# A tiled expert network on one core: half of the low-half weight tiles made by a VectorE subtraction instead of a ScalarE negation and an adding DMA

## Chip, core and metric

The kernel runs on one core of a Trainium2 chip. Its metric is the device time of one execution in microseconds (us). Three runs of the kernel before took 1112.21, 1112.51 and 1117.79 us; the median is 1112.51 us.

## What is computed

The program has three stages, each of which needs the whole of the one before it.

```python
attn_out = _attn_ref(q, k, v)                 # 4 x 8 heads, 768 tokens, head size 64, decaying state
x = attn_out.transpose(0, 2, 1, 3).reshape(3072, 512)
h = x @ w_in                                  # 512 -> 2048
x = np.where(h > 0, h, np.exp(np.minimum(h, 0)) - 1) @ w_out     # 2048 -> 512
logits = x @ w_gate                           # 3072 x 8 experts
...                                           # all logits sorted; a token goes to the best expert that
...                                           # still has room (3072 / 8 = 384 tokens each)
for e in range(8):                            # each expert: 512 -> 1024 -> 512 on its 384 tokens
    h = np.maximum(x[mask_e] @ w1[e], 0.0)
    out[mask_e] = h @ w2[e]
```

Which expert a token gets depends on an order over all logits, so the products are done in more than one float32r pass: each operand is kept as a high half (its rounding to float32r) and a low half (what the rounding left), and a product is the sum high x high + low x high + high x low.

## The kernel before, in words

**Order of the work.** `body` builds the program with generators (threads). Each yields the engine that it wants and the tiles that it needs, and `Sched` picks the thread that can go first by the times that `Plan` keeps: `Plan.cost` and `Plan.pe_cost` say how long an instruction takes, and `Plan.note` (line 153) books it. For a DMA `note` adds the bytes divided by a rate to one common DMA clock (line 168). The result is one fixed order on each engine; on the chip an engine works its queue in that order, and an instruction whose operand is late holds all behind it. So a changed cost in `Plan` moves instructions everywhere a DMA is waited for. All recorded operations have line 199 in the profile, since `Engine.__getattr__` issues them; tiles tell them apart.

**First part (0 to about 690 us).** Attention (`sc`, `A`, `py`, `pu`) and the first network (`ph`, `e`, `gH`/`gL`, `px`) over 12 blocks of 256 tokens. Its weights come in as 64-bit numbers (`rw`), are narrowed by three VectorE operations each, and split into `w1H`/`w1L`, `w2H`/`w2L`. From about 100 us TensorE (PE) is full.

**Expert part (about 690 us to the end).** `route(ph)` (line 850) finds, for one expert after the other, which expert fills next and with which tokens. It is a chain on VectorE (DVE): six digits, each with a compare `c`, a product `pc` on PE, `nums`, `num`, a second product into `pc`, `ind`, a product `pj`, `jd` and the next `xd`. It ends with the expert's number `es` and, through `listing`, its token list `idx`. Phases 0 to 6 run this chain, phase 7 is a short rest. `load_experts` (line 1095) lets the SP queue read `es` and then load the expert's weights as eight tiles of 512 KB, `e1R` and `e2R` in turn, into a ring of five buffers (`RAWS`, tag `raw`). `splits` (line 1116) makes the halves of each tile: ACT copies `x` to the high half `h`, ACT writes `-h` to the low half `l`, and a DMA from the GpSimd (POOL) queue adds `x` to `l` in place. The ring buffer is free again when that DMA has read it. `fetch` (line 1142) gathers the expert's tokens (`xg`) by indirect DMA, PE transposes them (`pt`), ACT and DVE split them (`xTH`, `xTL`). `ffn_first` (PE, `eh`), `ffn_mid` (ACT `hH`, DVE `hL`), `ffn_second` (PE, `po`) and `outs` (`o`, scatter to `out_dram`) do the expert's network: 96 `eh` and 72 `po` matmuls for each expert. The digit matmuls of routing stand in PE's queue between them.

The lines that matter: 

```python
h, l = (wp.tile(shp, F32R, tag=t, ...) for t in tags)     # splits, line 1125
copy("ACT", h, x)
ACT.activation(l, h.bitcast(F32), AF.Copy, scale=-1.0)
POOL.dma_start(l.bitcast(F32), x, accum_op=OP.add)
```

Of the kernel before, what the change touches and what calls it, by code (L numbers as in the profile page):

```python
# [12 lines left out]
F32 = mybir.dt.float32  # L13
# [4 lines left out]
AF = mybir.ActivationFunctionType  # L18
OP = mybir.AluOpType
# [68 lines left out]
class Plan:  # L88
# [64 lines left out]
    def note(self, eng, op, out, ins):  # L153
        o = out.tensor.name
        start = max([self.free[eng]] + [self.ready.get(x.tensor.name, 0.0) + self.gap(x.tensor.name, eng) for x in ins])
        if eng != "PE" or self.writer.get(o) != "PE":
            start = max(start, self.used.get(o, 0.0) + 140)
        if eng == "PE":
            end = start + self.pe_cost(op, ins, start)
            if start > self.free[eng] + 20:  # L160
                end += 100
        else:
            end = start + self.cost(eng, op, out, ins)
        self.free[eng] = end
        self.writer[o] = eng
        if "dma" in op:
            nb = self.size(out if out.space != "DRAM" else ins[0]) * P * 4
            self.dma = max(self.dma, end + 600) + nb / 360.0
            end = self.dma + 1300
        for x in ins:  # L170
            k = x.tensor.name
            self.used[k] = max(self.used.get(k, 0.0), end)
        self.used[o] = max(self.used.get(o, 0.0), end)
        self.ready[o] = max(self.ready.get(o, 0.0), end) if "dma" in op or eng == "PE" else end
# [107 lines left out]
def on(eng, *needs, when=None, rank=None):  # L282
    return eng, needs, when, rank
# [3 lines left out]
def body(ctx: ExitStack, tc, qkv, w_in, w_out, w_gate_t, w1, w2, cst, rc, rmat, out, dbg=None):  # L287
# [3 lines left out]
    PE, ACT, DVE, POOL, SP = (  # L291
        Engine(e, n, plan)
        for e, n in ((nc.tensor, "PE"), (nc.scalar, "ACT"), (nc.vector, "DVE"), (nc.gpsimd, "POOL"), (nc.sync, "SP"))
    )
# [20 lines left out]
    def copy(eng, o, i):  # L315
        if eng == "ACT":
            ACT.activation(o, i, AF.Copy)
        else:
            engines[eng].tensor_copy(o, i)
# [793 lines left out]
    def set_free(p):  # L1113
        return did["rest"] > 4 if p == 0 else did["late_x"] if p == 1 else did["p2e"] >= nf * (p - 1)

    def splits():
        for p in range(E):
            for q in range(8):
                i = q // 2
                yield on("ACT", when=lambda: did["loaded"] > 8 * p + q and set_free(p) and (p > 0 or q < 2 or did["gather"]))  # L1120
                x = weights[(p, q)]
                nm, shp = (("w1", [P, KD, 256]), ("w2", [P, 2, DM]))[q % 2]
                tags = [f"{nm}{h}{i + 4 * (p % 2)}" for h in "HL"]
                yield on("ACT", x, wp.slot(tags[0]))
                h, l = (wp.tile(shp, F32R, tag=t, name=f"{nm}{t[2]}{p}_{i}") for t in tags)
                copy("ACT", h, x)
                yield on("ACT", h)
                ACT.activation(l, h.bitcast(F32), AF.Copy, scale=-1.0)
                yield on("POOL", l)
                POOL.dma_start(l.bitcast(F32), x, accum_op=OP.add)  # L1130
                weights[(p, q)] = (h, l)
                did["split"] += 1

# [143 lines left out]
    sched.add(4, ffn_second())  # L1277
    sched.add(5, ffn_first())
    sched.add(6, splits())
    sched.add(7, load_experts())  # L1280
    sched.run()
# [35 lines left out]
```

## Time and profile before

| | us |
|---|---|
| median of three runs | 1112.51 |
| the profiled execution, its own time | 1109.6 |
| its span, first to last instruction | 1107.8 |
| PE busy in the span | 1010.9 (91%) |
| DVE busy | 736.8 (67%) |
| ACT busy | 422.1 (38%) |
| POOL busy | 258.0 (23%) |

The profiled execution lies 2.9 us under the median of the runs, and 1.8 us of it lie outside its span. A page of the profile gives busy times for each engine, the span in 40 slices of 27.7 us, the DMA queues, and the chain of waits that ended last. Queries on the trace give the same for a stretch of time, group the instructions by tile and shape, and list who waited for whom.

### The profile page before, as it was taken

Reading aid. Unit: us, or ns where it says so; the run is one execution under the profiler, and the core shown is the slowest. Engines: PE = TensorE matmul, PEld = TensorE weight load, DVE = VectorE, ACT = ScalarE, POOL = GpSimd, SP = SyncE. Lnnn points to the kernel's source line nnn. Section 1 sums busy time; section 2 is a strip of 40 time slices with the busy share of each in tenths; the row PEclk is TensorE's granted clock in tenths of the full one; section 3 lists DMA queues with packets and bytes.
Section 4 is the critical chain, followed back from the end, with each engine's and each line's share of the span. In section 5 each row is a group of like instructions: output and inputs, shape, how many; then the busy total and the mean of one; then the engine's idle time right before and its main releaser. Section 6 shows DMA issues by size and latency. Waiting matters only on the chain.

```text
span 1107.8 us, 17734 instructions
## 1 busy us (share of the span) xinstructions
PE 1010.9 (91%) x6899; PEld 847.4 (76%) x6899; DVE 736.8 (67%) x1853; ACT 422.1 (38%) x639; POOL 258.0 (23%) x250
## 2 busy tenths in 40 slices
PE   4779899999999999999999999959798898996996
PEld 3657687978787878787879899748586676786885
DVE  4989877898989888866574655567465565662210
ACT  3536423323232333323233344055353545545531
POOL 4665421211211212110000000032232324333321
PEclk8789999999999999999999999989898989998999
DMA  9743232020202020201010000099797979989860
GB/s 317 258 158 115 101 109 96 1 95 2 96 1 87 9 81 16 74 24 65 32 57 1 20 1 12 20 261 241 192 238 194 243 195 224 252 235 259 195 151 29
DMA packets 60582, 131.80 MB, mean 119 GB/s; under 512 B 4689, under 2 KB 29265, under 8 KB 60369
## 3 DMA queue, kind: packets, MB, share of 16 engines
q1 hardware_dynamic: 47440, 84.52, 22.7%
q0 software_dynamic: 13056, 46.14, 19.2%
q8 instruction: 54, 0.88, 0.3%
q14 instruction: 32, 0.25, 0.1%
HBM read 84.51 MB, written 12.58 MB: 88 GB/s over the span
## 4 chain that ended last, share of the span: by engine, by line
PE 61%; DVE 15%; DMA 13%; issue 6%; ACT 2%; POOL 1%; SPq 0%; POOLq 0%; DVEq 0%; ACTq 0%
PE px L199 19%; PE ph L199 18%; PE eh L199 8%; PE po L199 8%; DVE junk L199 6%; PE py L199 4%; DMA e2R<-in_w_dram 3%; DVE n_rw L199 3%; DMA rw<-in_moe_w_in_dram 3%; DMA e1R<-in_w_dram 2%; DVE e L199 2%; DMA xg<-xd,idx 2%; DMA w1L<-e1R 2%; PE sc L199 1%; DVE gL L199 1%
## 5 line engine op out<-in xcount | busy, mean ns | idle before, releaser
L199 PE MATMUL ph<-yH,w1H 128*128 128x256 f32 x768 | 219.9, 286 | 8.1 <-DVE e L199 8.1
L199 PE MATMUL ph<-yL,w1H 128*128 128x256 f32 x768 | 216.0, 281 | 0.8 <-DVE yL L199 0.8
L199 PE MATMUL ph<-yH,w1L 128*128 128x256 f32 x768 | 215.9, 281 | 0.0
L199 PEld LDWEIGHTS ph<-yH,w1H 128*128 128x128 f32 x768 | 145.7, 190 | 14.5 <-DVE e L199 7.3
L199 PEld LDWEIGHTS ph<-yH,w1L 128*128 128x128 f32 x768 | 145.7, 190 | 1.6
L199 PEld LDWEIGHTS ph<-yL,w1H 128*128 128x128 f32 x768 | 145.5, 190 | 1.3 <-DVE yL L199 1.3
L199 PE MATMUL px<-w2H,gH 128*128 128x512 f32 x332 | 136.3, 411 | 8.8 <-DMA rw<-in_moe_w_in_dram 5.1
L199 PE MATMUL px<-w2H,gL 128*128 128x512 f32 x332 | 132.4, 399 | 1.7 <-DVE gL L199 1.7
L199 PE MATMUL px<-w2L,gH 128*128 128x512 f32 x332 | 132.9, 400 | 0.0
L199 DVE SCALAR_TENSOR_TENSOR junk<-x,wgb 128x512 f32<-128x512 f32 x160 | 128.0, 800 | 5.0 <-ACT x L199 1.2
L199 ACT ACTIVATE e<-ph 128x512 f32<-128x512 f32 x96 | 56.8, 592 | 195.5 <-PE ph L199 195.5
L199 DVE SCALAR_TENSOR_TENSOR hL<-eh,hH 128x384 fp32r<-128x384 f32 x64 | 35.6, 557 | 97.6 <-ACT hH L199 97.0
L199 ACT ACTIVATE gH<-e 128x512 fp32r<-128x512 f32 x83 | 52.3, 631 | 123.6 <-DVE e L199 115.0
L199 DVE SCALAR_TENSOR_TENSOR junkw<-wsum,wgb 128x512 f32<-128x512 f32 x128 | 89.4, 698 | 11.0 <-POOL wsum L199 8.4
L199 PE MATMUL eh<-xTH,w1H 128*128 128x384 f32 x256 | 91.5, 358 | 1.6 <-ACT xTH L199 1.6
L199 PE MATMUL eh<-xTL,w1H 128*128 128x384 f32 x256 | 90.1, 352 | 0.0
L199 PE MATMUL eh<-xTH,w1L 128*128 128x384 f32 x256 | 89.9, 351 | 0.0
L199 PE MATMUL po<-w2H,hH 128*128 128x512 f32 x192 | 80.5, 419 | 10.0 <-ACT hH L199 10.0
L199 PEld LDWEIGHTS px<-w2H,gH 128*128 128x128 f32 x332 | 63.3, 191 | 25.3 <-ACT gH L199 9.4
L199 POOL TENSOR_TENSOR qk<-qk,csb 128x512 f32<-128x512 f32 x23 | 32.0, 1392 | 212.3 <-DMA qk<-in_qkv_dram 212.3
L199 PE MATMUL po<-w2L,hH 128*128 128x512 f32 x192 | 79.8, 416 | 0.0
L199 PE MATMUL po<-w2H,hL 128*128 128x512 f32 x192 | 79.7, 415 | 0.0
(168 smaller groups left out, 1930.2 us busy)
## 6 DMA issues: line engine op xcount, KB each, us to landing
e1R<-in_w_dram SPq DMA_DIRECT2D x32, 512.0 KB, 6.3
e2R<-in_w_dram SPq DMA_DIRECT2D x32, 512.0 KB, 6.6
w1L<-e1R POOLq DMA_DIRECT2D x32, 512.0 KB, 7.3
w2L<-e2R POOLq DMA_DIRECT2D x32, 512.0 KB, 7.6
kv<-in_qkv_dram SPq DMA_DIRECT2D x24, 512.0 KB, 5.0
qk<-in_qkv_dram SPq DMA_DIRECT2D x23, 512.0 KB, 4.5
rw<-in_moe_w_in_dram SPq DMA_DIRECT2D x16, 512.0 KB, 10.3
rw<-in_moe_w_out_dram SPq DMA_DIRECT2D x16, 512.0 KB, 8.9
```

Source lines behind the costliest of these rows:

```text
L199: r = real(*args, **kw)
```

## The change

In `splits`, a tile whose index `i` is even (`i` runs 0 to 3 for each of `w1` and `w2`) gets its low half from one DVE subtraction `l = x - h`; for an odd `i` ACT and the adding DMA make it as before. So 32 of 64 negations (ACT) and 32 of 64 adding DMAs (POOL queue) go, and 32 subtractions of 128 x 1024 elements (DVE) come. In `Plan.note` the rate at which the planner lets a DMA move bytes changes from 360 to 150 (bytes per ns) for direct DMAs of POOL, and to 310 for all others.

```diff
@@ Plan.note
-            self.dma = max(self.dma, end + 600) + nb / 360.0
+            self.dma = max(self.dma, end + 600) + nb / (150.0 if op == "dma_start" and eng == "POOL" else 310.0)
@@ splits
                 copy("ACT", h, x)
-                yield on("ACT", h)
-                ACT.activation(l, h.bitcast(F32), AF.Copy, scale=-1.0)
-                yield on("POOL", l)
-                POOL.dma_start(l.bitcast(F32), x, accum_op=OP.add)
+                if i % 2 == 0:
+                    yield on("DVE", h)
+                    DVE.tensor_sub(l, x, h.bitcast(F32))
+                else:
+                    yield on("ACT", h)
+                    ACT.activation(l, h.bitcast(F32), AF.Copy, scale=-1.0)
+                    yield on("POOL", l)
+                    POOL.dma_start(l.bitcast(F32), x, accum_op=OP.add)
```

Both edits move instructions. First DVE in the third digit of routing phase 2, while expert 1's weights come in (`c_2`, `nums_2`, `ind_2`, `jd_2` are the digit's chain; `hL` and `xTL` belong to the expert network). Before:

```order
L199 TENSOR_TENSOR c_2_7714<-xd_1_7712,rmb 128x768
L199 TENSOR_TENSOR nums_2_7733<-pc_2_7725,rmb 128x32
L199 SCALAR_TENSOR_TENSOR hL_7723<-eh_7_7686,hH_7722 128x384
L199 TENSOR_REDUCE num_2_7745<-nums_2_7733 128x8
L199 SCALAR_TENSOR_TENSOR w_2_7749<-xd_1_7712,dig_7502 128x24
L199 TENSOR_TENSOR ind_2_7753<-pc_2_7725,rem 32x8
L199 TENSOR_REDUCE jd_2_7760<-pj_2_7756 128x1
```

and now:

```order
L199 TENSOR_TENSOR c_2_7721<-xd_1_7719,rmb 128x768
L199 TENSOR_TENSOR w1L_2_7729<-e1R_2_7539,w1H_2_7728 128x1024
L199 TENSOR_TENSOR nums_2_7750<-pc_2_7735,rmb 128x32
L199 TENSOR_REDUCE num_2_7752<-nums_2_7750 128x8
L199 TENSOR_TENSOR w2L_2_7733<-e2R_2_7615,w2H_2_7732 128x1024
L199 SCALAR_TENSOR_TENSOR w_2_7762<-xd_1_7719,dig_7507 128x24
L199 TENSOR_TENSOR ind_2_7764<-pc_2_7735,rem 32x8
```

Two subtractions stand between the steps of one digit. Of the 32, one stands in the token listing after phase 0, three in phase 1 and four in each of phases 2 to 6; the other eight come after routing.

Second PE around the product `pn` of the last routing chain, phase 6 (the digit behind `eh` and `po` is the expert, the next one the piece `f` of `eh`). Before:

```order
L199 MATMUL po4_2_9662<-w2L4_3_9530,hH39_10121 128x512
L199 LDWEIGHTS rmb_6594
L199 MATMUL pn6_10154<-g6_10140,rmb_6594 128x384
L199 MATMUL po4_2_9662<-w2H4_3_9529,hL39_10122 128x512
L199 MATMUL eh5_0_10168<-xTH5_9889,w1H5_0_9741 128x384
```

and now:

```order
L199 MATMUL po5_1_10149<-w2H5_0_9801,hH41_10152 128x512
L199 LDWEIGHTS rmb_6594
L199 MATMUL pn6_10185<-g6_10167,rmb_6594 128x384
L199 MATMUL po5_1_10149<-w2L5_0_9802,hH41_10152 128x512
L199 MATMUL po5_1_10149<-w2H5_0_9801,hL41_10153 128x512
L199 MATMUL po5_2_10150<-w2H5_0_9801,hH41_10152 128x512
L199 MATMUL po5_2_10150<-w2L5_0_9802,hH41_10152 128x512
L199 MATMUL po5_2_10150<-w2H5_0_9801,hL41_10153 128x512
L199 MATMUL eh5_2_10195<-xTH5_9893,w1H5_1_9870 128x384
```

Behind `pn` of phase 6 there stood 288 `eh` and 217 `po` matmuls, now 264 and 203: 24 and 14 have moved ahead of it. Between `pn` of phases 1 and 2 stood 87 `eh` and 65 `po`, now 61 and 54; in the four stretches after that together 360 and 276, now 397 and 301.

Third SP near the start of the program, where it loads the first network's weights (`rw`) and the attention blocks (`qk`, `kv`). Before:

```order
L199 DMA rw_211<-in_moe_w_in_dram 128x4x256
L199 DMA rw_213<-in_moe_w_in_dram 128x4x256
L199 DMA qk_234<-in_qkv_dram 128x1024
L199 DMA kv_235<-in_qkv_dram 128x1024
```

and now:

```order
L199 DMA qk_223<-in_qkv_dram 128x1024
L199 DMA kv_224<-in_qkv_dram 128x1024
L199 DMA rw_229<-in_moe_w_in_dram 128x4x256
L199 DMA rw_231<-in_moe_w_in_dram 128x4x256
```

One block's load goes ahead of a weight load there, and behind one at a second place; the rest of SP's order, the whole expert part in it, is the same. On PE, DVE, ACT and POOL the order of the first 130 us or so changes with it, and DVE takes two `w1L` subtractions and two of the `rw` scalings of that part from POOL (ACT takes two more scalings), and hands one `qk` and one `kv` product to POOL.

## Rows read from the trace of the kernel before

**Rows 1.** The page, parts 1 and 2: busy times; 40 slices, DMA in tenths.
```profile
PE 1010.9 (91%) x6899; PEld 847.4 (76%) x6899; DVE 736.8 (67%) x1853; ACT 422.1 (38%) x639; POOL 258.0 (23%) x250
...
DMA  9743232020202020201010000099797979989860
```

**Rows 2.** Stretches: routing phases 0 to 6 (from m<-lg on), two more.
```profile
core 0: us, PE busy (x) PEld busy (x) DVE busy (x) ACT busy (x) POOL busy (x), PEclk, DMA share, GB/s
690.50:728.20 37.70, 35.81 (x207) 26.05 (x205) 23.67 (x103) 5.40 (x7) 1.15 (x1) 1.00 0.20 70
728.20:762.70 34.50, 24.54 (x158) 19.22 (x159) 22.46 (x95) 15.44 (x20) 9.55 (x10) 0.85 1.00 242
762.70:809.80 47.10, 41.15 (x239) 33.13 (x238) 26.50 (x107) 21.95 (x28) 13.72 (x17) 0.89 0.82 210
809.80:856.60 46.80, 40.74 (x250) 33.39 (x249) 26.84 (x109) 22.34 (x29) 13.60 (x17) 0.93 0.85 220
856.60:903.70 47.10, 40.45 (x241) 32.03 (x240) 26.51 (x108) 22.02 (x28) 13.63 (x17) 0.93 0.85 212
903.70:945.40 41.70, 38.25 (x244) 30.92 (x243) 26.29 (x108) 23.10 (x30) 14.20 (x17) 1.00 0.93 233
945.40:986.90 41.50, 39.16 (x245) 32.42 (x243) 24.76 (x97) 23.01 (x30) 14.22 (x17) 0.96 0.90 225
986.90:1030.00 43.10, 34.37 (x188) 29.62 (x187) 16.59 (x57) 21.84 (x29) 13.35 (x14) 0.88 1.01 268
1030.00:1064.00 34.00, 34.00 (x171) 30.77 (x170) 6.12 (x11) 21.15 (x27) 10.47 (x15) 1.00 0.89 205
```

**Rows 3.** DMA queues from 720 to 1064 us: packets, MB, share of 16 engines.
```profile
q0 software_dynamic: 12362, 43.83, 59.4%
q1 hardware_dynamic: 25888, 34.08, 30.1%
```

**Rows 4.** The SP queue's own waits: us in total, times, longest.
```profile
SPq L199 <- DMA w1L<-e1R: 119.1, 18, 10.8
SPq L199 <- DVE sel L199: 74.8, 4, 26.0
```

**Rows 5.** Who waited for whom in the expert part, same columns.
```profile
DVE hL L199 <- ACT hH L199: 97.0, 37, 15.5
...
ACT w1H L199 <- DMA e1R<-in_w_dram: 42.0, 8, 11.6
```

**Rows 6.** The chain that ended last: start us, us, link.
```profile
832.10 10.96 DMA e2R<-in_w_dram
```

**Rows 7.** Busy time of stretch 20 to 120 us, columns of rows 2.
```profile
20.00:120.00 100.00, 79.72 (x540) 65.77 (x540) 96.03 (x124) 49.72 (x85) 64.31 (x42) 0.85 0.51 181
```

**Rows 8.** DVE groups, first 130 us: count, busy us, mean ns.
```profile
L199 DVE TENSOR_SCALAR rw<-rw 128x512 f32<-128x512 f32 x2 | 2.0, 980 | 0.0
...
L199 DVE TENSOR_TENSOR kv<-kv,csb 128x512 f32<-128x512 f32 x1 | 1.4, 1450 | 0.0
```

**Rows 9.** keepL, subtraction of two SBUF inputs: ns min/median/max, first, last start.
```profile
L199 DVE TENSOR_TENSOR keepL<-e,keepH x13: 691/693/694, 647.6 to 686.1; 128x512 fp32r<-128x512 f32 x13
```

**Rows 10.** The same for gL in the first 130 us, where POOL computes too.
```profile
L199 DVE TENSOR_TENSOR gL<-e,gH x9: 677/685/1784, 41.0 to 123.0; 128x512 fp32r<-128x512 f32 x9
```

**Rows 11.** Groups in the expert part, columns as in rows 8.
```profile
L199 DVE SCALAR_TENSOR_TENSOR hL<-eh,hH 128x384 fp32r<-128x384 f32 x64 | 35.6, 557 | 97.6 <-ACT hH L199 97.0
L199 ACT ACTIVATE w1L<-w1H 128x1024 fp32r<-128x1024 f32 x32 | 33.8, 1058 | 0.7
```

**Rows 12.** DVE in time, a routing digit: start us, us, instruction, idle before.
```profile
836.02 0.19 DVE L199 TENSOR_TENSOR nums<-pc,rmb 128x32 f32<-128x32 f32 x1 [0.71 <-PE pc L199]
...
836.85 0.15 DVE L199 TENSOR_TENSOR ind<-pc,rem 32x8 bf16<-32x8 f32 x1 [0.31 <-PE pc L199]
```

**Rows 13.** The chain in the stretch where PE is never idle.
```profile
1030.59 4.24 PE eh L199 x24
1034.83 4.20 PE po L199 x18
```

## Prediction

> **What bounds the kernel now.** Begin with the page: PE is busy 91% of the span, DVE 67%, and the DMA slices are low in the middle but 7 to 9 tenths from about 690 us on [rows 1]. So the place to read is the expert part, and the view to read it in is a table of stretches, one for each routing phase [rows 2]. Between 762.7 and 903.7 us a phase takes 47 us; the two after that take 41.7 and 41.5. In the stretch from 1030 us, where routing is over and the weights are in, PE is never idle at the full clock. Before it PE loses time: summed over the seven stretches from 728.2 to 1030, their lengths less PE's busy time make 301.8 - 258.7 = 43.1 us, and a granted clock of 0.85 to 0.96 in six of them adds about 19.6 us (busy time times what the clock lacks). These 63 us are all that the part can give.
>
> Who takes them? The 16 DMA engines are 82% to all but fully occupied [rows 2], and more by POOL's queue than by the loads: in 344 us it has 59.4%, the loads' queue 30.1% [rows 3]. That is 204.3 us for 43.83 MB, so 2.44 us of all 16 engines for one adding DMA of 0.524 MB if its bytes cost as much as the queue's others, against 1.59 us for a load. SP, which issues the loads, waits 119.1 us for the adding DMAs of `w1` tiles to give ring buffers back, and 74.8 us for routing [rows 4]. Late loads of `w1` tiles hold ACT for 42.0 us, and while ACT's queue stands, so does its `hH`, for which DVE waits 97.0 us in all [rows 5]. One link of the chain shows a late load: issued at 832.10, it is waited for over 10.96 us [rows 6]. Routing is the other pacemaker: a digit's steps on DVE and PE answer each other, and all other DVE work stands in between.
>
> **The change, part by part.** I make the sum against the profiled execution, 1109.6 us, which lies 2.9 us under the median of the runs.
>
> *The first part.* Stretch 20 to 120 us has DVE at 96% [rows 7]. The new order gives DVE two subtractions (0.69 each, as `keepL` [rows 9]) and two scalings of 0.98, and takes away two products, one of 1.45 [rows 8] and one that I count as 0.69 like a subtraction of its size: **+1.2 us**. PE idles 20 us in the same 100, so the reordered loads can also give some back or cost more: I keep -5 to +6.
>
> *The subtraction.* No row has one of 1024 columns. With 512 columns it takes 693 ns [rows 9], and a DVE operation of 384 columns (`hL`) takes 557 ns [rows 11], so a column costs about 1.06 ns and 1024 make 1.23 us. Beside POOL's arithmetic the same operation reached 1784 ns [rows 10], 1.1 us more. Bounds: 0.7 and 3.6 us (twice the worst). I take **1.23**, since POOL only issues DMAs and clears one column in the expert part. The Trainium skill (SBUF — State Buffer, Who interferes with whom) says that a VectorE instruction with two SBUF inputs contends with a GpSimd instruction that reads SBUF, and infers that descriptor writing is not hit; the trace agrees with its first half, with 1784 ns where POOL computes, and no row shows the second. If issuing did block it, 24 subtractions at 1.1 us more would add 26 us and the sum would come to about nothing.
>
> *What of it lies on the path.* 24 subtractions come before routing ends: one in the listing ahead of phase 1, three in phase 1, four in each of phases 2 to 6. They stand in the waits of a digit, which under load are some 0.3 to 0.7 us long [rows 12]. So about half of each, 0.6 us, is hidden, and 0.6 is paid: 2.4 us a phase.
>
> *The phases without the adding DMAs.* 32 of them go: 32 x 2.44 = 78 us of 308 us of DMA time, a quarter. Half the ring buffers come back after the subtraction instead of after a DMA's landing. Then the stalls by late loads should mostly go, and a phase is DVE's work plus the waits of the bare chain. DVE is busy 26.2 us in the mean of phases 2 to 6, and in phase 0, which ran with DMA at 0.20, it idled 37.7 - 23.7 = 14.0 us [rows 2]. That makes 40.2, with the subtractions 42.6. Phase 1 had few stalls by loads and gets 3 x 0.6 = **+1.8 us**. The cover for half of each subtraction is the wait for PE's answer; where PE answers at once it is paid in full.
>
> *What PE does meanwhile.* An `eh` matmul takes 4.24/24 = 0.177 us and a `po` 4.20/18 = 0.233 [rows 13]. PE's order has 24 `eh` and 14 `po` fewer behind the last routing phase: 7.5 us of work moved ahead into stretches where PE now idles. Its price there is PE's time: in phases 3 to 6 the mean busy time is 39.65 us, and 37 `eh` and 25 `po` more over the four add 3.1, together 42.75, a little over DVE's 42.6. So phases 2 to 6 make 42.6 + 4 x 42.75 = 213.6 us against 224.2 today: **-10.6 us**.
>
> *The tail.* From 986.9 to the span's end are 120.9 us. The 7.5 us are gone from it, and the first stretch there has 43.10 - 34.37 = 8.7 us of idle PE and 34.37 x 0.12 = 4.1 us of clock, with DMA at 1.01 [rows 2]; I take three quarters of these 12.8 us back, 9.6. **-17.1 us.** The clock's levels are 1.2 and 2.4 GHz; it fell in this part after PE had stood, so it comes back with the stall.
>
> *Costs at nothing.* ACT loses 32 negations of 1.06 us [rows 11]; it is busy 22 to 23 us of a phase, so they pay only by letting `hH` go sooner. POOL loses 32 DMA issues; it is busy some 14 us of a phase [rows 2].
>
> Sum: 1.2 - 10.6 + 1.8 - 17.1 = -24.7 us, 1084.9 for the profiled execution; with 2.9 for the median, **1088 us**. The terms' bounds (first part -5 to +6, hiding all or nothing of 24 subtractions, the tail's stall wholly or by half back) give this case 1075 to 1104.
>
> **The rivals.** *PE becomes the bound.* The subtractions vanish in the waits, DVE idles less, and a phase is as long as PE's work. By matmul busy time there is no room for this (42.75 us). By weight loads there is: in phases 3 to 6 they are busy 32.2 us on average, and where PE never idles they fill 30.77 of 34.00, 90.5% [rows 2], so the work is worth 35.6 us, with 3.1 more 38.7, say 39. Then phases 2 to 6 give 195 - 224.2 = -29.2, phase 1 nothing, the tail -7.5 - 12.8 = -20.3, the first part +1.2: -48.3, **1064 us**. For it: the digit waits are many and the planner places by readiness. Against: DVE's 14 us of waits in phase 0, with hardly any other work. The Trainium skill (Perfetto Trace Analysis, Identifying the Most-Contended Engine) says that matmul busy time is a poor measure of headroom and weight-load busy time a good one; by the first this rival could not be, by the second it ends near 1064. The trace agrees as far as it goes: from 1030 us on PE counts as busy for all of 34.00 us, at a rate of matmuls that phases 2 to 6 don't reach.
>
> *The phases stay.* What lengthens phases 2 to 4 is DVE's own queue, not DMA: they keep their mean of 44.84, plus 2.4. That is +12, +1.8, +1.2 and -17.1: -2.1, **1110 us**. For it: phases 5 and 6, at 41.6, had DMA at 0.9 too.
>
> *DVE as the new holder (slower).* A subtraction waits on DVE for ACT's copy, thus for the load, and holds the digit behind it, `hL` and `xTL`, and with them PE and SP (which waits for routing). Then nothing is hidden and the stalls remain: phases 2 to 6 at 44.84 + 4 x 1.23 = 49.8, +24.7; phase 1 +3.7; first part +1.2; tail -17.1: +12.5, **1125 us**. It decides from where phases 2 to 6 average 47.3 us, 2.4 over today, since the other terms give 12.2 us for five. Against: loads will land sooner, and ACT's in-order queue already held `hL` in this way.
>
> That the change doesn't do what it says is small: the subtraction frees its ring buffer, but the odd tiles still need their adding DMA, and a phase that waits for one of these waits as before. It lies between the forecast and 1110.
>
> **How the numbers follow.** A measurement here can tell about 0.5%, 5.6 us, from no change. Forecast 0.52, PE as the bound 0.25, the phases stay 0.13, DVE as holder 0.10. The first two are faster by over 0.5%: 0.77; the third is the same: 0.13; the last slower: 0.10. The range runs from just under the PE case to the case of no change, 1062 to 1112, and leaves out the slower case and some of the faster one's low end.
>
> **What would show it.** Right: `w1L<-e1R` and `w2L<-e2R` as DVE operations, 16 each at about 1.23 us; 32 adding DMAs; phase starts (`m<-lg`) 43 us apart; SP's wait for `w1` tiles' adding DMAs under half of 119.1 us; about 104 us from the end of phase 6 to the span's end, at a clock near 1. Wrong: phases of 47 us or more with DVE waiting at the subtractions for ACT's copies; subtractions near 2 us or longer; a first part over 6 us longer.

## Result and profile after

The changed kernel takes 1082.72 us (median of four runs, 1080.62 to 1084.07) where the kernel before took 1115.05 (1112.21 to 1117.79) beside it: ratio 0.9709, 95% interval 0.9671 to 0.9746, faster by 2.9%. In two later comparisons the ratio was 0.980 (0.975 to 0.984) and 0.976 (0.973 to 0.980). The changed kernel's medians there are 1084.58 and 1082.89; the kernel before is the one that scatters, its runs reach from 1100.18 to 1120.53. The forecast was 1088, in a range of 1062 to 1112. The profiled execution took 1080.62 us, its span is 1078.9, 28.9 us shorter than that of before.

The page first, to be held against [rows 1]: PE and ACT are busy for less time, DVE for longer, and the slices of DMA from the 28th to the 39th read 5 to 8 where 6 to 9 stood.

```profile
PE 1000.9 (93%) x6899; PEld 843.6 (78%) x6899; DVE 775.0 (72%) x1887; ACT 391.6 (36%) x609; POOL 225.3 (21%) x214
...
DMA  9752241112020203030201000008568667568752
```

The stretches, columns as in [rows 2]: routing phases 0 to 6, which now start at 695.7, 733.6, 768.8, 809.0, 849.8, 891.6 and 933.6 us, then the first 45 us behind them.

```profile
695.70:733.60 37.90, 35.85 (x207) 26.01 (x205) 23.53 (x102) 5.18 (x7) 0.00 (x0) 1.00 0.22 70
733.60:768.80 35.20, 27.95 (x168) 22.03 (x169) 25.82 (x98) 12.77 (x17) 6.87 (x7) 0.81 0.58 155
768.80:809.00 40.20, 34.30 (x202) 27.80 (x202) 30.08 (x110) 17.75 (x23) 10.00 (x13) 0.83 0.73 201
809.00:849.80 40.80, 40.80 (x259) 33.92 (x258) 30.78 (x111) 18.90 (x26) 10.67 (x13) 1.00 0.70 191
849.80:891.60 41.80, 41.80 (x266) 35.03 (x265) 30.80 (x111) 19.18 (x27) 10.30 (x13) 1.00 0.73 202
891.60:933.60 42.00, 42.00 (x266) 35.11 (x265) 31.69 (x113) 18.81 (x26) 11.25 (x12) 1.00 0.64 183
933.60:973.80 40.20, 40.20 (x257) 33.48 (x256) 30.01 (x103) 17.07 (x25) 11.18 (x13) 1.00 0.68 189
973.80:1018.80 45.00, 44.24 (x249) 38.74 (x248) 22.64 (x64) 22.65 (x32) 13.89 (x17) 1.00 0.77 214
```

From 809.0 to 973.8 us PE's busy time is the stretch's length, at the full clock. Before, in none of the phases 2 to 6 was it so.

The DMA queues from 720 to 1064 us, against [rows 3]:

```profile
q0 software_dynamic: 8208, 28.58, 35.8%
q1 hardware_dynamic: 26032, 34.35, 30.6%
```

POOL's queue takes 123.2 us of the 16 engines instead of 204.3, for 15.25 MB or 29 tiles less: 2.8 us for one adding DMA, against 1.6 us for a load.

The waits behind [rows 4] and [rows 5]: first of SP's queue, then of ACT and DVE from 690 us on.

```profile
SPq L199 <- DVE sel L199: 66.5, 4, 18.6
SPq L199 <- DMA w1L<-e1R: 65.4, 9, 9.3
...
SPq L199 <- DVE w2L L199: 22.5, 6, 6.7
```

```profile
DVE hL L199 <- ACT hH L199: 56.9, 36, 5.9
ACT w1H L199 <- DMA e1R<-in_w_dram: 11.2, 4, 9.9
```

ACT's wait for late `w1` tiles fell from 42.0 to 11.2 us, DVE's for `hH` from 97.0 to 56.9. And the subtractions themselves (minimum, median, maximum in ns), all 32 between 1205 and 1228 ns:

```profile
L199 DVE TENSOR_TENSOR w1L<-e1R,w1H x16: 1210/1218/1228, 730.7 to 1046.8; 128x1024 fp32r<-128x1024 f32 x16
```

```profile
L199 DVE TENSOR_TENSOR w2L<-e2R,w2H x16: 1205/1216/1221, 737.1 to 1047.9; 128x1024 fp32r<-128x1024 f32 x16
```

The first part got longer, as stretch 20 to 120 us shows beside [rows 7]: DVE is as busy as before, PE has 10.9 us less.

```profile
20.00:120.00 100.00, 68.78 (x494) 59.39 (x495) 96.75 (x126) 48.04 (x82) 57.48 (x38) 0.85 0.52 183
```

**One way to add it up.** From the start of routing to the span's end, in three parts (phases 0 and 1, phases 2 to 6, the tail behind them), take PE's busy time times the granted clock: this is PE's work at full clock. Before and after it is 339.1 and 340.6 us, the same but for rounding. So what counts is the rest, the time that PE loses: 78.2 us of 417.3 before, 42.6 of 383.2 after. The granted clock is given to two digits, which makes a loss uncertain by up to about 2 us (0.005 of some 355 us of busy time). The rows of after are these; those of before are the second block.

```profile
695.70:768.80 73.10, 63.80 (x375) 48.04 (x374) 49.34 (x200) 17.95 (x23) 6.87 (x7) 0.91 0.39 111
768.80:973.80 205.00, 199.10 (x1243) 165.34 (x1243) 153.36 (x544) 91.70 (x125) 53.41 (x64) 0.97 0.70 193
973.80:1078.90 105.10, 92.14 (x483) 80.93 (x481) 36.03 (x82) 41.67 (x58) 24.13 (x33) 0.97 0.59 158
```

```profile
690.50:762.70 72.20, 60.35 (x365) 45.27 (x364) 46.14 (x197) 20.84 (x26) 10.70 (x11) 0.93 0.58 152
762.70:986.90 224.20, 199.75 (x1211) 161.89 (x1209) 130.90 (x522) 112.43 (x145) 69.36 (x85) 0.94 0.87 220
986.90:1107.80 120.90, 102.42 (x525) 90.89 (x523) 27.17 (x75) 49.57 (x67) 30.31 (x40) 0.93 0.68 173
```

### The profile page after: what moved, and what is told of

Its sections match the earlier page's. It is cut to its first block, busy times and chain, and to the rows that moved or that the text cites. A ratio compares the mean times of both kernels' runs of the same rounds, so it can differ in the third digit from the quotient of the medians.

```text
span 1078.9 us, 17649 instructions
## 1 busy us (share of the span) xinstructions
PE 1000.9 (93%) x6899; PEld 843.6 (78%) x6899; DVE 775.0 (72%) x1887; ACT 391.6 (36%) x609; POOL 225.3 (21%) x214
## 4 chain that ended last, share of the span: by engine, by line
PE 71%; DVE 14%; issue 5%; ACT 1%; POOL 1%; DMA 0%; POOLq 0%; DVEq 0%
PE px L199 20%; PE ph L199 20%; PE eh L199 11%; PE po L199 10%; DVE junk L199 5%; PE py L199 4%; DVE e L199 2%; DVE n_rw L199 2%; PE sc L199 1%; PE pt L199 1%; DVE rw L199 1%; PE pc L199 1%; DVE gL L199 1%; PE lacc L199 1%; ACT e L199 1%
## 5 line engine op out<-in xcount | busy, mean ns | idle before, releaser
L199 PEld LDWEIGHTS ph<-yH,w1H 128*128 128x128 f32 x768 | 146.3, 191 | 27.1 <-ACT rw L199 10.9
L199 DVE SCALAR_TENSOR_TENSOR junkw<-wsum,wgb 128x512 f32<-128x512 f32 x128 | 89.4, 698 | 10.9 <-POOL wsum L199 8.4
L199 PE MATMUL eh<-xTH,w1L 128*128 128x384 f32 x256 | 90.5, 353 | 0.8 <-DVE w1L L199 0.8
L199 ACT ACTIVATE hH<-eh 128x384 fp32r<-128x384 f32 x64 | 31.5, 491 | 148.8 <-PE eh L199 127.2
L199 DVE SCALAR_TENSOR_TENSOR hL<-eh,hH 128x384 fp32r<-128x384 f32 x64 | 35.6, 556 | 60.0 <-ACT hH L199 56.9
L199 PE MATMUL po<-w2L,hH 128*128 128x512 f32 x192 | 77.4, 403 | 0.0
L199 DVE TENSOR_SCALAR e<-e 128x512 f32<-128x512 f32 x85 | 40.1, 471 | 51.0 <-ACT e L199 51.0
```

What stands on the lines that cost most here:

```text
L199: r = real(*args, **kw)
```

## Experiments

The table gives the results of all; each run is told below. "Stretch" is the time from the start of routing to the span's end, "lost" its length less PE's work as above.

| kernel | median us | ratio to before (95%) | routing starts | stretch | phases 2 to 6 | tail | lost |
|---|---|---|---|---|---|---|---|
| before | | | 690.5 | 417.3 | 224.2 | 120.9 | 78.2 |
| changed | 1082.72 | 0.971 (0.967 to 0.975) | 695.7 | 383.2 | 205.0 | 105.1 | 42.6 |
| rates only | 1119.06 | 1.006 (1.003 to 1.009) | 694.6 | 420.8 | 189.1 | 158.8 | 81.6 |
| subtraction only | 1083.92 | 0.976 (0.970 to 0.981) | 690.4 | 392.6 | 210.7 | 106.3 | 52.5 |
| rates 150 and 360 | 1078.47 | 0.971 (0.965 to 0.976) | 689.6 | 387.3 | 205.8 | 105.2 | 47.2 |
| no add | 1072.86 | 0.965 (0.959 to 0.970) | 696.4 | 376.3 | 189.0 | 112.7 | 38.9 |
| changed, again | 1084.58 | 0.980 (0.975 to 0.984) | 696.8 | 384.4 | 204.5 | 105.7 | 46.5 |
| all by subtraction | 1091.75 | 0.986 (0.981 to 0.991) | 689.7 | 399.1 | 220.8 | 99.4 | 58.6 |
| traffic kept | 1140.59 | 1.031 (1.026 to 1.036) | 694.1 | 444.7 | 203.2 | 165.7 | 106.1 |
| buffers held | 1090.11 | 0.984 (0.979 to 0.989) | 696.0 | 392.5 | 205.8 | 114.3 | 50.8 |
| changed, third | 1082.89 | 0.976 (0.973 to 0.980) | 694.2 | 386.1 | 204.4 | 107.1 | 46.0 |
| 150 and 360, again | 1078.90 | 0.973 (0.969 to 0.978) | 691.7 | 383.3 | 205.4 | 103.2 | 44.0 |
| ends by subtraction | 1080.72 | 0.974 (0.970 to 0.977) | 691.5 | 388.7 | 203.3 | 104.4 | 52.8 |
| subtraction on POOL | 1106.06 | 0.997 (0.994 to 1.000) | 694.0 | 412.3 | 221.5 | 111.8 | 72.4 |

**Rates only.** The kernel before, with the edit in `Plan.note` and nothing else.

```diff
-            self.dma = max(self.dma, end + 600) + nb / 360.0
+            self.dma = max(self.dma, end + 600) + nb / (150.0 if op == "dma_start" and eng == "POOL" else 310.0)
```

> The kernel before with the new rates in Plan.note alone: all 64 adding DMAs stay, no DVE subtraction. Theory A (the gain comes from the subtractions: fewer adding DMAs, ring buffers back sooner; the rates only cost the 5.2 us of the first part): first routing starts near 695.7 us as in the changed kernel, against 690.5 before, phases 2 to 6 stay near 44.8 us each, the time is 0 to 1% over before (about 1115 to 1125). Theory B (the new rates let the planner place work where it really fits, and that makes the gain): phases 2 to 6 near 41 us, ratio 0.97 to 0.98.

The time is as theory A has it, 0.6% over before. Its phases are not: 2 to 6 fell to 189.1 us, lower than theory B asked for, and the tail took it all back. Two rows say why: phases 2 to 6, and the stretch from 1020 us, where the DMA engines have a share of 0.99.

```profile
767.50:956.60 189.10, 171.44 (x1038) 135.52 (x1038) 132.10 (x533) 81.46 (x107) 53.96 (x65) 0.88 0.77 193
...
1020.00:1064.00 44.00, 41.46 (x208) 36.22 (x209) 9.33 (x16) 23.14 (x30) 11.10 (x15) 1.00 0.99 252
```

The planner now lets routing run and puts the experts' matmuls behind it (1038 in phases 2 to 6 instead of 1211), but all 64 adding DMAs are still there, and PE loses 81.6 us instead of 78.2. A shorter phase alone is therefore no gain.

**Subtraction only.** The changed kernel with `nb / 360.0` for every DMA, as before.

> The changed kernel with the old rate, 360 for every DMA: only the subtractions are new. Theory A: the first part is that of before (routing from 690.5 us), phases 2 to 6 near 41 us, ratio about 0.966, that is about 5 us faster than the changed kernel. Theory B: phases 2 to 6 at 44 us or more, ratio 0.98 to 1.0.

Theory A in the main: without any new rate 25 us of the stretch are gained. The ratio came out at 0.976 and not 0.966, though, since with the old rate phases 2 to 6 stay at 210.7 us and PE loses 52.5 us. The two new rates make the stretch 6 to 9 us shorter (383.2 to 386.1 in three profiles of the changed kernel) and let routing start 4 to 6 us later; that the edit in `Plan.note` gains anything on the whole is not shown, the intervals of 0.971 and 0.976 overlap.

**Rates 150 and 360.** Only POOL's direct DMAs get the new rate.

```diff
-            ... nb / (150.0 if op == "dma_start" and eng == "POOL" else 310.0)
+            ... nb / (150.0 if op == "dma_start" and eng == "POOL" else 360.0)
```

> The changed kernel with 360 in place of 310 for all DMAs that are not direct ones of POOL; 150 stays for those. The order of the first part is then that of before, since POOL issues no direct DMA there. Theory A, on the first part: the 5.2 us come from the order that 310 gives; routing starts at 690.5 us and the time is 5 us under the changed kernel, ratio about 0.966. Rival: the expert part needs 310 as well (its loads are planned too early with 360), and what the first part gives back is lost there: ratio 0.97 or more.

Routing starts at 689.6 us, as expected: the first part's loss comes from the order that 310 gives. All traces bear it out: in the stretch 20 to 120 us PE is busy 68.1 to 70.7 us in the seven with 310, and 77.2 to 80.4 us in the seven with 360. The stretch after it is 387.3 us, 1 to 4 us over the changed kernel's, and the ratio, 0.971, is the changed kernel's and not theory A's 0.966: by the ratio the rival stands. Beside the run before, on the same chip, 150 in place of 360 for the adding DMAs gains 5 us, once half of them are gone.

**No add.** ACT makes `-h` for the even tiles too, and nothing is added.

```diff
                 if i % 2 == 0:
-                    yield on("DVE", h)
-                    DVE.tensor_sub(l, x, h.bitcast(F32))
+                    yield on("ACT", h)
+                    ACT.activation(l, h.bitcast(F32), AF.Copy, scale=-1.0)
```

> The changed kernel, but ACT writes -h to the low half of the even tiles, as for the odd ones, and neither a subtraction nor an adding DMA follows: the low half of 32 of 64 tiles lacks its x. It has the 32 adding DMAs gone at no cost on DVE. Theory of the prediction (each subtraction in a digit is half hidden, 0.6 us of it paid): phases 2 to 6 are 2.4 us shorter than in the changed kernel, some 38.5 us, and the time about 14 us under it, ratio 0.958. Rival (PE sets the phases' length, the subtractions are hidden wholly): phases 2 to 6 stay near 41 us and the ratio near 0.971; should ACT's negations hold hH, it is over that.

The phases are as the theory has them, the time lies between the two. Phases 2 to 6 fall by 16 us, to 37.8 each, which is the length of phase 0; the tail gives 7.6 back, and PE loses 4 to 8 us less than in the three profiles of the changed kernel. By spans the subtractions cost 6.2 us, by medians of different chips 10 to 12: 0.3 to 0.5 us for each of the 24 that come before routing ends, less than half of the 1.22 us that one lasts, net of the ACT negations that stand in their place here. Phase 2, and phases 3 to 6 together:

```profile
771.00:807.90 36.90, 33.46 (x208) 26.95 (x207) 25.86 (x107) 21.30 (x27) 10.04 (x13) 0.91 0.79 222
...
807.90:960.00 152.10, 151.99 (x977) 125.67 (x976) 104.96 (x417) 85.12 (x110) 36.38 (x44) 1.00 0.73 196
```

PE is full in phases 3 to 6 here too. They are shorter than the changed kernel's 164.8 us because the fixed order puts 977 matmuls into them instead of 1042 (counted in one window). So some 13 of the 16 us are matmuls that stand elsewhere, and only phase 2 shows the subtractions in DVE's chain. And since all 64 negations are on ACT here, what ACT is spared is not the gain.

**The changed kernel, again,** beside the three that follow:

> The changed kernel as it is, to stand on one chip beside the three that follow. Ratio 0.967 to 0.975; first part 695.7 us, from there to the span's end 383 us (417.3 before).

The stretch was as expected; the ratio, 0.980, lies above the range named, beside a kernel before that took 1108.42 us in this comparison.

**All by subtraction.** On top of the rates 150 and 360:

```diff
-                if i % 2 == 0:
+                if True:
                     yield on("DVE", h)
                     DVE.tensor_sub(l, x, h.bitcast(F32))
```

> All 64 low halves by a DVE subtraction (no negation, no adding DMA left), with the rates 150 and 360 of the run with the split rates; that one's stretch from the start of routing to the span's end was 387.3 us at 1076.9. Theory C (what the DMAs still hold is worth more than the subtractions cost; a subtraction costs about 0.3 us on the path, as the run without adding DMAs gave: 383.2 - 376.3 = 6.9 us for 24): 24 more subtractions before routing ends cost some 7 us, the DMA queue of POOL falls under 15% of the 344 us and the stretch gets 10 to 20 us shorter: 370 to 378 us, time 1060 to 1068. Rival D (DVE is now what the phases wait for, every further subtraction is paid in full, 1.23 us each): 24 x 1.23 = 30 us more, and little to regain: 400 us or more, time 1090.

Theory C is refuted. The time is Rival D's, at a smaller price: the stretch is 11.8 us longer than with half the subtractions (15.8 against the later profile of that kernel), not 30. The stretch of phases 2 to 6, and the queues from 720 to 1064 us:

```profile
768.60:989.40 220.80, 205.42 (x1239) 167.62 (x1238) 173.61 (x558) 71.94 (x107) 38.09 (x45) 0.94 0.38 128
```

```profile
q1 hardware_dynamic: 25888, 34.08, 29.9%
q0 software_dynamic: 3600, 11.80, 9.4%
```

DMA is at 0.38, far from full, DVE is busy 173.61 of 220.80 us, and PE, which lost 11.5 us in these phases of the run it builds on, loses 27.7. That DVE holds it up is likely, but not shown: of the 15.4 us in which PE is idle there, 2.1 wait directly for a digit's step on DVE, and 7.4 for a gather of tokens, where the run that it builds on has 2.3.

```profile
PE pt L199 <- DMA xg<-xd,idx: 7.4, 6, 3.0
```

Without adding DMAs POOL's queue takes 32.3 us; before, it took 204.3 with 32.03 MB more, 61 tiles: 2.8 us an adding DMA again.

**Traffic kept.** The changed kernel, with an adding DMA that reads `h` instead of the ring buffer:

```diff
                     DVE.tensor_sub(l, x, h.bitcast(F32))
+                    yield on("POOL", l)
+                    POOL.dma_start(l.bitcast(F32), h.bitcast(F32), accum_op=OP.add)
```

> The changed kernel with an adding DMA of the same size put back behind each of the 32 subtractions: it adds the high half h to l, so these low halves are x and not x - h. It reads h, not x, so the ring buffer still comes free after the subtraction. Theory E (what the change saves is the time of the 16 DMA engines): from the start of routing to the span's end the stretch is back at 410 us or more (383.2 in the changed kernel, 417.3 before), ratio 1.0 or over. Rival F (it is the ring buffers that come back sooner): the stretch stays under 395 us, ratio 0.975 to 0.985.

Theory E, beyond what it asked for: 444.7 us, longer than before. The phases have 203.2 us, near the changed kernel's 205.0, the tail has 165.7. With the rates the same, four kernels make a square:

| phases 2 to 6 / tail / lost, us | 64 adding DMAs | 32 adding DMAs |
|---|---|---|
| no subtraction | 189.1 / 158.8 / 81.6 (rates only) | 189.0 / 112.7 / 38.9 (no add) |
| 32 subtractions | 203.2 / 165.7 / 106.1 (traffic kept) | 205.0 / 105.1 / 42.6 (changed) |

Down a column, 20 subtractions lengthen the phases by 14 to 16 us. Across a row, 32 adding DMAs leave the phases' length alone, lengthen the tail by 46 to 61 us and cost PE 43 to 64. But phases of one length hold unequal work. The rows of phases 2 to 6 and of the tail, first of no add, then of traffic kept:

```profile
771.00:960.00 189.00, 185.46 (x1183) 152.62 (x1182) 130.81 (x522) 106.42 (x137) 46.42 (x57) 0.98 0.74 201
960.00:1072.70 112.70, 102.70 (x546) 92.26 (x544) 29.86 (x78) 52.47 (x71) 28.90 (x40) 0.96 0.59 161
...
769.90:973.10 203.20, 176.01 (x1072) 141.91 (x1072) 145.98 (x545) 75.06 (x103) 60.20 (x72) 0.89 0.76 197
973.10:1138.80 165.70, 135.58 (x651) 119.39 (x649) 46.00 (x80) 60.66 (x81) 40.34 (x55) 0.92 0.74 185
```

With 64 adding DMAs PE gets through 1038 and 1072 matmuls in the phases, with 32 through 1183 and 1243. By length less work it loses 31 and 35 us more there, over half of what the 32 DMAs cost it, and the matmuls left over lengthen the tail. Nor do the two costs simply add up: beside 64 adding DMAs the subtractions cost PE 24.5 us, beside 32 only 4 to 8. Traffic kept even loses more than the kernel before (106.1 against 78.2), at a lower DMA share in the phases (0.76 against 0.87). Its low halves need a subtraction and then a DMA, and in the tail PE waits 12.1 us for three of them; what part of the excess comes from this is not shown.

**Buffers held.** The changed kernel, with a small DMA that reads the ring buffer:

```diff
                     DVE.tensor_sub(l, x, h.bitcast(F32))
+                    yield on("POOL", l)
+                    POOL.dma_start(l[:, 0, :64].bitcast(F32), x[:, 0, :64], accum_op=OP.add)
```

> The changed kernel with a small adding DMA behind each of the 32 subtractions, 64 columns of x onto the same 64 columns of l (which are then 2x - h): POOL issues as many DMAs as before, the ring buffer is held until the small DMA has landed, and nearly no bytes move. Theory E: the stretch from the start of routing stays within 6 us of 383.2, ratio 0.97 to 0.98. Rival F: most of the gain goes, the stretch is 400 us or longer, ratio 0.985 or over.

Nearer to theory E, though over its 6 us: 392.5 against 383.2 to 386.1 in three profiles of the changed kernel, 6 to 9 us. The ratio, 0.984, lies between the two ranges named, with 0.980 for the changed kernel beside it. F is refuted as the main cause. This run also has a DMA behind each subtraction, so the 52 us of the stretch that it lies under traffic kept are the price of the bytes, with the order that the planner makes for them. What part of the 6 to 9 us is the ring buffer, POOL's issuing, or the small DMAs themselves (POOL's queue went from 35.8% to 38.8% of the 344 us) was not told apart.

**Candidates for a faster kernel.** On one chip: the changed kernel a third time, the rates 150 and 360 again, and two that build on the latter.

> The changed kernel as it is, beside the three that follow: ratio 0.968 to 0.98, stretch from the start of routing to the span's end 383 to 385 us.

> The run with the rates 150 and 360 once more, on one chip with the changed kernel. If the first part's order alone makes the difference (routing starts 6 us earlier, the stretch after it is 2 to 4 us longer, 387.3 against 383.2 and 384.4): 2 to 6 us faster than the changed kernel, ratio to before 0.003 to 0.006 lower. Rival: the difference lies within what one kernel scatters by, ratios equal within 0.002.

The changed kernel's stretch was 386.1 us, a little over the 383 to 385. The medians are 1082.89 and 1078.90, 4.0 us apart, as 1078.47 had stood under 1082.72 and 1084.58 from other chips. But the runs of the second reach from 1076.80 to 1086.55, and the ratios' intervals overlap: likely faster by 0.4%, not shown. Nor do the profiles place the difference as expected: routing starts 2.5 us earlier, not 6, and the stretch after it is 2.8 us shorter, not 2 to 4 us longer. In the first part the rows of stretch 20 to 120 us have 77.17 us of PE, in place of 70.69 in the changed kernel on the same chip; the changed kernel comes second:

```profile
20.00:120.00 100.00, 77.17 (x540) 63.36 (x540) 96.48 (x125) 49.75 (x85) 64.37 (x42) 0.90 0.51 182
...
20.00:120.00 100.00, 70.69 (x505) 61.21 (x506) 98.38 (x128) 49.12 (x83) 57.64 (x39) 0.81 0.53 186
```

**Ends by subtraction.** More subtractions for the first and the last two experts:

```diff
-                if i % 2 == 0:
+                if i % 2 == 0 or p in (0, 6, 7):
```

> The split rates, and all eight low halves of the first expert and of the last two by DVE subtraction: 12 adding DMAs fewer, where DVE does not run the bulk of the routing chain. If DMA still delays the ends (in phase 1 it is at 1.00, and the tail loses 2.1 us of PE and 1.7 us of clock in its first 45 us): phase 1 keeps its 36.4 us or loses up to 3, the tail falls from 105.2 to 101 or 102, time 3 to 6 us under the split rates. Rival (PE's work sets the tail, it is busy 42.89 of 45.00 us there): within 2 us of the split rates, or slower where the subtractions meet the chain of phase 1, by up to 4 x 0.8 us.

A miss: the tail is 104.4, where 103.2 and 105.2 stand in the two profiles it builds on, and phase 1 grew to 41.6 us on top (36.3 and 36.4 there). The rival was right, and it underrated phase 1.

**Subtraction on POOL.** Also on top of the rates 150 and 360:

```diff
-                    yield on("DVE", h)
-                    DVE.tensor_sub(l, x, h.bitcast(F32))
+                    yield on("POOL", h)
+                    POOL.tensor_tensor(l, x, h.bitcast(F32), op=OP.subtract)
```

> The split rates, but the 32 subtractions on POOL instead of DVE; no adding DMA for these tiles, as before. Theory G (a subtraction costs about 0.8 us in a phase because DVE must do it: phases 2 to 6 make 189.0 us without any, 205.0 with 20, 220.8 with 40): off DVE the phases fall back to 189 to 195 us and the stretch from the start of routing to 378 to 382 us, 5 to 9 us under the split rates. Rival H (POOL's arithmetic holds up DVE's as in the first part, where a subtraction of DVE reached 1784 ns against 685, and the low halves come later): DVE operations of 351 or 557 ns show longer ones, phases 2 to 6 stay at 205 us or over, time equal to the split rates or slower.

Rival H: 1106 us, nearly all of the gain is lost, though the adding DMAs are gone. A subtraction takes POOL 2.5 us:

```profile
L199 POOL TENSOR_TENSOR w1L<-e1R,w1H 128x1024 fp32r<-128x1024 f32 x16 | 41.2, 2577 | 91.8 <-ACT w1H L199 91.7
L199 POOL TENSOR_TENSOR w2L<-e2R,w2H 128x1024 fp32r<-128x1024 f32 x16 | 39.9, 2494 | 5.7 <-ACT w2H L199 5.7
```

And DVE suffers beside it. The compares `c` from phase 2 to the end of routing, minimum, median and maximum in ns, with the rates 150 and 360 and then with the subtractions on POOL, and `hL` of the latter:

```profile
L199 DVE TENSOR_TENSOR c<-xd,rmb x30: 550/560/959, 770.0 to 961.4; 128x768 bf16<-128x768 bf16 x20, 128x1536 bf16<-128x1536 bf16 x10
```

```profile
L199 DVE TENSOR_TENSOR c<-xd,rmb x30: 548/560/3334, 781.6 to 983.2; 128x768 bf16<-128x768 bf16 x20, 128x1536 bf16<-128x1536 bf16 x10
L199 DVE SCALAR_TENSOR_TENSOR hL<-eh,hH x38: 539/557/559, 767.1 to 989.0; 128x384 fp32r<-128x384 f32 x38
```

`c` has both inputs in SBUF and reaches 3334 ns, though its median stays; `hL` has one in PSUM and stays at 557. The Trainium skill (SBUF — State Buffer, Who interferes with whom) says that a VectorE operation with two SBUF inputs contends with a GpSimd one that reads SBUF, and that one with at most one SBUF input doesn't, outside the modes that use both ports; the two rows agree with it. The exception matters: `di` has one input in SBUF and two constants, and some of its 36 are hit as hard, as the same two runs show. In which mode it ran no run shows.

```profile
L199 DVE TENSOR_SCALAR di<-key x36: 167/172/326, 731.0 to 937.8; 128x24 uint32<-128x24 uint32 x36
...
L199 DVE TENSOR_SCALAR di<-key x36: 160/169/2372, 733.2 to 964.7; 128x24 uint32<-128x24 uint32 x36
```

In sum DVE is busy 166.31 us in phases 2 to 6, with no subtraction of weights, where no add has 130.81, and PE waits 10.6 us there for `c`. What the later low halves add to this was not told apart.

```profile
773.00:994.50 221.50, 195.24 (x1192) 159.08 (x1192) 166.31 (x525) 91.46 (x122) 103.00 (x83) 0.95 0.62 170
```

The Trainium skill's inference on the same page, that descriptor writing does not hit such an operation, is borne out by the changed kernel, in whose trace subtractions run while POOL issues DMAs (start us, us, first DVE, then POOL), and none of the 32 took over 1228 ns.

```profile
785.41 1.22 DVE L199 TENSOR_TENSOR w1L<-e1R,w1H 128x1024 fp32r<-128x1024 f32 x1
786.89 1.22 DVE L199 TENSOR_TENSOR w2L<-e2R,w2H 128x1024 fp32r<-128x1024 f32 x1
```

```profile
785.38 1.02 POOL L199 DMA_DIRECT2D w2L<-e2R  x1
786.70 1.04 POOL L199 DMA_INDIRECT out_dram<-o,idx  x1 [0.30 <-issue]
```

## Why the prediction was right, and where its steps were off

The direction, the cause and the time were right; of 28.9 us the sum had 24.7. That it came so near is partly luck: the first part took 4.0 us more than its term, which hides about half of the 8.6 us by which phases 2 to 6 gave more. And the upper end of 1104 does not come out of the terms: their bounds added up (4.8 us for the first part, some 14 if nothing is hidden, 3.2 for the tail) reach about 1110. By its own terms:

| term | predicted | measured |
|---|---|---|
| first part | +1.2 | +5.2 |
| phase 0 | 0 | +0.2 |
| phase 1 | +1.8 | +0.7 |
| phases 2 to 6 | -10.6 | -19.2 |
| tail | -17.1 | -15.8 |

*The cause: confirmed.* It is the bytes of the adding DMAs. Put back behind the subtractions, the traffic takes more than the whole gain away; holding the buffers and issuing as many DMAs with nearly no bytes takes 6 to 9 of some 34 us; the rates alone gain nothing; and with all negations back on ACT (no add) the time is shorter still. That the bytes cost by the time of the 16 engines, and not by the delay until each low half has landed, is argued from the DMA share and from the shorter waits for loads; no run tells the two apart. One adding DMA was priced at 2.44 us by the mean of its queue and takes 2.8, so 90 us of DMA time went, not 78. SP's wait for `w1` tiles' DMAs fell to 65.4 us, a little short of the half that was named.

*The subtraction: 1.23 predicted, 1.22 measured.* That 0.6 us of each is paid seems not far off for the phases: 14 to 16 us for 20 subtractions are 0.7 to 0.8 each. But that is chance: most of the 16 us lies in phases 3 to 6, where PE is full with and without the subtractions, and where the number of matmuls in the phase makes its length. And a longer phase is not all lost, because PE works meanwhile and the tail gets shorter: 0.3 to 0.5 us of each reach the end.

*Phases 2 to 6: the largest error, 8.6 us.* Phase 2 had DVE's price, 42.6, and took 40.2 (38.9 and 39.2 in the two later profiles); there DVE is busy 30.1 us, with 4 subtractions in it where the sum's 26.2 had none, and idle 10.1 in place of the 14.0 that the sum took from phase 0 and kept fixed. It is the fixed 14.0 that failed: without subtractions (no add) DVE is idle for 11.0 us of phase 2, which takes 36.9, so the four still cost 2 to 3 us. Phases 3 to 6 had PE's price, 4 x 42.75 = 171.0 us, and took 164.8. The mechanism was right: PE is busy for all of them. What failed is the step "in phases 3 to 6 the mean busy time is 39.65 us". That is busy time at granted clocks of 0.93, 0.93, 1.00 and 0.96 [rows 2], and it has to be taken times the clock: (37.9 + 37.6 + 38.25 + 37.6) / 4 = 37.8. With the 3.1 us for the work moved in this makes 40.9, measured 41.2. The move itself was counted well: 62 matmuls, and the four stretches show 1048 instead of 980.

*The rival "PE becomes the bound"* was thus right in its mechanism for phases 3 to 6 and wrong in its price. It took weight loads at 90.5% of a full stretch, as where PE is never idle in the tail, and came to 38.7 us a phase. In phases 3 to 6 PE is never idle either, and the weight loads fill 137.5 of 164.8 us, 83.5%: the share that means "full" was not the same for the two mixes of matmuls. The Trainium skill (Perfetto Trace Analysis, Identifying the Most-Contended Engine) prefers weight loads to busy matmul time as a measure of headroom. Here matmul busy time times the granted clock gave 40.9, weight loads 38.7, and 41.2 came out.

*DVE as the new holder* didn't come with four subtractions a phase. With eight PE loses 27.7 us in phases 2 to 6 instead of 11.5, which fits it, though PE waited there more for gathers than for DVE.

*The tail* is 15.8 us shorter where the sum said 17.1, by its two parts: PE's work in it fell from 95.3 to 89.4 us (5.9, forecast 7.5), the time it loses there from 25.6 to 15.7 (9.9, forecast 9.6). How the gain falls on phases and tail hangs on the planner, too (189.1 and 158.8 us with the rates alone), so that both terms came near is partly luck.

*The first part: +1.2 failed, within its bounds.* It was priced as DVE work, and DVE's busy time in 20 to 120 us did grow by only 0.7 us. But the new order makes PE wait for `e` of DVE, 2.8 us before and 16.3 now, by the waits of 20 to 130 us:

```profile
PE ph L199 <- DVE e L199: 2.8, 2, 2.5
...
PE ph L199 <- DVE e L199: 16.3, 2, 10.8
```

PE had 10.9 us less of busy time in 20 to 120 us, and made up part of it before routing started.

## What to carry to other kernels

Multiply TensorE's busy time by the granted clock before it is used as the price of work; then add up what PE loses over the whole rest of the program, since single stages can get shorter (189 us for 224 here) and the program longer. A DMA that adds in place took 2.8 us of all 16 engines here, against 1.6 for a load of the same size, so some of them can be traded for work on an engine with waits to fill, but only up to a point: 32 subtractions gained 31 to 34 us of the stretch, 64 gave 12 to 16 of it back. And when a planner's constant changes, look at every stage that it reorders, not only at the one it was meant for.

## Not expected

The same subtraction on POOL is no cheap way out: it takes 2.5 us there, it stretches single compares of DVE to as much as 3.3 us, and with it the phases are as long (221.5 us) as with twice the subtractions on DVE (220.8). And phases 2 to 6 without subtractions take 189.0 us with 32 adding DMAs and 189.1 with 64. That is no sign that the DMAs are free there: PE does 1183 matmuls in the one and 1038 in the other. How long routing took was set by DVE's work and by what the planner put beside it; the DMAs' time shows in the work that PE gets done meanwhile, and the tail pays for the rest.
